# A decode attention kernel: the mask of the sliding-window units computed on chip from the identity, in place of two software-queued DMAs

## Chip, cores and metric

One core of a Trainium2 chip runs the whole program; the other cores are idle. The metric is the device time of one execution in microseconds (us), as the median over several executions. One run profiled by the hardware profiler goes with each kernel.

## The reference

Two independent decode attentions, A and B, with one query token for each of 4 batches, 32 query heads on 8 key/value heads, head size 128 and a cache of 8192 positions. A uses the whole cache, B its last 2048 positions. The outputs are concatenated.

```python
def _B_ref(x, k_cache, v_cache, wq, wo):          # A: the same without the window
    W = min(4096, max(256, Sk // 4))              # 2048
    q = (x @ wq).reshape(B, Sq, Hq, Dh) ...
    k = jnp.repeat(k_cache[:, :, Sk - W:, :], rep, axis=1)
    v = jnp.repeat(v_cache[:, :, Sk - W:, :], rep, axis=1)
    p = _softmax(jnp.einsum("bhqd,bhkd->bhqk", q, k) * (Dh ** -0.5), axis=-1)
    o = jnp.einsum("bhqk,bhkd->bhqd", p, v)
    return o ... @ wo                             # out: (4, 1, 1024) bf16
```

## The kernel before

The work is cut into 20 units: 4 of B, one for each batch, then 16 of A, one for each batch and pair of key/value heads. For every unit, SyncE loads 4.19 MB of K and 4.19 MB of V; TensorE transposes K (line 283), multiplies the scores, VectorE and ScalarE make the softmax, TensorE multiplies by V. K and V have two buffers each, so a load is issued as soon as the unit before the last has released its buffer.

In the K layout used here, a partition of the score tile belongs to one of two heads of a pair. Before the maximum over the partitions is taken, the columns of the other head are pushed to -1e30 by adding a mask. For A (MASKA) the two kinds of partitions are the lower and the upper half, which memsets can write. For B (MASKB) they alternate, even and odd. The kernel before wrote the rows into a helper tile MK in halves and let two DMAs from GpSimd's queue (software-queued: an instruction on GpSimd writes their descriptors) spread the rows over every second partition:

```python
def dve_addmask(u):                                     # first reader of the mask
    ...
    return dve.tensor_tensor(out=M1m[:, 0:n], in0=..., in1=MASK[P][:, 0:n], op=AluOpType.add)
    # waits: the scores' maximum, and in unit 0 also ("mk", 1), ("mka",)

def pool_mask0(pool):
    mkv = MK[:, :].rearrange("p (g s h) -> p g s h", g=NSEG, s=2)
    pool.memset(mkv[0:64, :, 0, :], 0.0)
    pool.memset(mkv[0:64, :, 1, :], -BIG)
    pool.memset(mkv[64:128, :, 0, :], -BIG)
    return pool.memset(mkv[64:128, :, 1, :], 0.0)
op("pool", pool_mask0, inc=("mk0",))
# ... pool_mask1 (MASKA), pool_setup0 (ones, zeros of RQ, OT_sb, oacc, PT, Wo_sb),
#     pool_setup1 (the identities ident and identf by affine_select), pool_perm

def dve_msk(dve):
    idv = ident[0:NR, 0:NR].rearrange("p (h b) -> p h b", h=C)
    dve.tensor_reduce(out=MSK[:, :], in_=idv, axis=AX.X, op=AluOpType.max)
    return dve.tensor_reduce(out=SEL[:, :], in_=idv.rearrange("p h b -> p b h"), axis=AX.X, op=AluOpType.max)
op("dve", dve_msk, waits=[("setup",)], inc=("msk",))
for sh in range(2):
    ...                                                 # destination: every second partition of MASKB
    def mfn(pool, dst_ap=dst_ap, sh=sh):
        return pool.dma_start(out=dst_ap, in_=MK[64 * sh:64 * sh + 64, :])
    op("pool", mfn, waits=[("mk0",)], inc=("mk", sh))
```

The set-up of the queries waits for the identity too: TensorE transposes x with it, projects x with WQ, and the first V load is issued when the B part of WQ, which lies in V's buffer, has been used.

Of the kernel before, what the change touches and what calls it, by code (L numbers as in the profile page):

```python
# [7 lines left out]
F32 = mybir.dt.float32  # L8
I32 = mybir.dt.int32
ACTF = mybir.ActivationFunctionType  # L10
AX = mybir.AxisListType
# [3 lines left out]
def bass_concat_heads__gqa_block_cached__sliding_block_cached__decode_kernel(  # L15
# [18 lines left out]
    REP = HQ // HKV  # L34
# [4 lines left out]
    NSEG = 4  # L39
    TS = NT // NSEG  # L40
    C = 2 * REP
# [4 lines left out]
    BIG = 1.0e30  # L46
# [13 lines left out]
    WQ = [A_wq, B_wq]  # L60
# [12 lines left out]
    with ExitStack() as es:  # L73
        block = es.enter_context(nc.Block())

        def sb(name, shape, dt):
            return es.enter_context(nc.sbuf_tensor(name, shape, dt))
# [4 lines left out]
        def sm(name):  # L82
            return es.enter_context(nc.semaphore(name))
# [6 lines left out]
        ident = sb("ident", [128, 128], BF16)  # L90
# [3 lines left out]
        RQ = [sb("RQ%d" % P, [128, Bn, NSEG, 2, 2 * C], BF16) for P in range(2)]  # L94
        RQc = sb("RQc", [128, 2, NSEG, 2, 2 * C], BF16)
        permE = sb("permE", [128, 2, 2, 64], BF16)
        MK = sb("MK", [128, NSEG * C], F32)
        MASK = [sb("MASKA", [128, C], F32), sb("MASKB", [128, NSEG * C], F32)]
        M1 = sb("M1", [128, NSEG * C], F32)
        M1m = sb("M1m", [128, NSEG * C], F32)  # L100
# [14 lines left out]
        ORx = sb("ORx", [C * Bn, C, C, 128 // C], BF16)  # L115
        MSK = sb("MSK", [C * Bn, C], BF16)
        SEL = sb("SEL", [C * Bn, Bn], BF16)
        OL = sb("OL", [128, C, Bn], BF16)
        oacc = sb("oacc", [Bn, D], F32)
        osb = sb("osb", [Bn, 2, D], BF16)  # L120
# [5 lines left out]

        names = ["k0", "k1", "kh", "v0", "v1", "vl0", "vl1", "vl2", "vl3", "vl4", "wl0", "wl1", "wl2", "wl3", "wl4", "wl5", "wl6", "wl7", "x0", "x1", "w0", "w1", "wo",
                 "out0", "out1", "out2", "Tq", "Td", "Ta", "S", "PV", "Ed", "Ea", "Eq", "vs", "sub", "exp", "otr", "otp",
                 "ocp", "Ef", "fin0", "fin1", "ar1", "SM", "msk", "pset", "setup", "pm0", "pm1", "oc", "ocB", "mk0", "mk", "mka", "perm", "rq"]
        sems = {n: sm("s_" + n) for n in names}  # L130

        K_sbf = K_sb.bitcast(F32)
# [6 lines left out]
        def sem_of(key):  # L139
            t = key[0]  # L140
            if t in ("K", "Kh"):
                return sems["k%d" % (key[1] % 2)]
            if t in ("V", "Vh"):
                return sems["v%d" % (key[1] % 2)]
            if t == "T":
                j = jobs[key[1]]
                return sems["Tq" if j["turn"] is None else "Td" if j["eng"] == "dve" else "Ta"]
            if t == "pm":
                return sems["pm%d" % key[2]]
            if t == "KH":  # L150
                return sems["kh"]
            if t in ("VL", "WL", "x", "out", "fin"):
                return sems["%s%d" % (t.lower(), key[1])]
            if t == "WQ":
                return sems["w%d" % key[1]]
            if t == "E":
                if jobs[key[1]]["turn"] is None:
                    return sems["Eq"]
                return sems["Ed"] if jobs[key[1]]["eng"] == "dve" else sems["Ea"]
            return sems["vs" if t in ("max", "maxc", "sum", "rcp", "os") else t]  # L160

        DMA_KEYS = ("K", "Kh", "KH", "V", "Vh", "VL", "WL", "x", "out", "WQ", "wo", "mk")

        plan = {e: [] for e in ("sp", "pe", "act", "dve", "pool")}
        turn = [None]
# [1 line left out]
        def op(eng, fn, waits=(), inc=None, bump=None):  # L167
            waits = list(waits)
            if not (eng == "pe" and turn[0] is not None):
                waits = [w for w in waits if w is not None]  # L170
            t = turn[0] if eng == "pe" or (eng in ("dve", "act") and turn[0] is not None and turn[0] >= T0P) else None
            plan[eng].append(dict(fn=fn, waits=waits, inc=inc, turn=t, bump=bump))
# [4 lines left out]
        def new_job(kind, eng):  # L177
            idx = len(jobs)
            step = 2 if kind == "OT" else 1
            bank = (jobs[-1]["bank"] + step) % NBK if jobs else 0  # L180
            jobs.append(dict(kind=kind, idx=idx, bank=bank, prev=bank_last.get(bank), eng=eng, turn=turn[0]))
            bank_last[bank] = idx
            return idx
# [7 lines left out]
        def kbank(idx):  # L191
            return KTB[jobs[idx]["bank"]]
# [180 lines left out]
        def pe_job_OL(tn):  # L373
            idx = ol_idx[tn] = new_job("OL", "dve")
            bk = kbank(idx)

            def fn(pe):
                ins = None
                for r in range(C):
                    ins = pe.matmul(out=bk[:, r * Bn:(r + 1) * Bn], lhsT=ORx[:, r, :, :].rearrange("p o i -> p (o i)"),  # L380
                                    rhs=SEL[:, :], start=True, stop=True)
                return ins
            op("pe", fn, waits=[("E", ot_idx[tn]), bankfree(idx)], inc=("T", idx))

            def efn(dve):
                return dve.tensor_copy(out=OL[:, :, :].rearrange("p r b -> p (r b)"), in_=bk[:, 0:NR])
            return dict(eng="dve", fn=efn, waits=[("T", idx)], inc=("E", idx))

        def pe_job_OPJ(tn):
# [3 lines left out]
            def fn(pe):  # L393
                ins = None
                for i in range(C):
                    ins = pe.matmul(out=bk[0:Bn, 0:D], lhsT=OL[:, i, :], rhs=Wo_sb[:, i, :],  # L396
                                    start=(i == 0), stop=(i == C - 1))
# [9 lines left out]
        def ncol(u):  # L407
            return NSEG * C if units[u]["P"] == 1 else C
# [21 lines left out]
        def dve_addmask(u):  # L430
            n, P = ncol(u), units[u]["P"]

            def fn(dve):
                return dve.tensor_tensor(out=M1m[:, 0:n], in0=M1[:, 0:n] if P == 1 else M1c[:, :], in1=MASK[P][:, 0:n], op=AluOpType.add)  # L434
            return dict(eng="dve", fn=fn, waits=[("max", u, 1) if P == 1 else ("maxc", u)] + ([("mk", 1), ("mka",)] if u == 0 else []), inc=("pm", u, 0))

        def pool_ar1(u):
            n = ncol(u)
# [80 lines left out]
                w.append(("otr", 2 * tn - 2))  # L519
            return dict(eng="pool", fn=lambda pool: pool.tensor_copy(out=OTp[:, :, :], in_=OT_sb[:, P, q, :, :]), waits=w, inc=("otp", tn))  # L520

        def pool_mask0(pool):
            mkv = MK[:, :].rearrange("p (g s h) -> p g s h", g=NSEG, s=2)
            pool.memset(mkv[0:64, :, 0, :], 0.0)
            pool.memset(mkv[0:64, :, 1, :], -BIG)
            pool.memset(mkv[64:128, :, 0, :], -BIG)
            return pool.memset(mkv[64:128, :, 1, :], 0.0)
        op("pool", pool_mask0, inc=("mk0",))

        def pool_mask1(pool):  # L530
            pool.memset(MASK[0][0:64, 0:REP], 0.0)
            pool.memset(MASK[0][0:64, REP:C], -BIG)
            pool.memset(MASK[0][64:128, 0:REP], -BIG)
            return pool.memset(MASK[0][64:128, REP:C], 0.0)
        op("pool", pool_mask1, inc=("mka",))

        def pool_setup0(pool):
# [6 lines left out]
            pool.memset(oacc[:, :], 0.0)  # L544
            pool.memset(PT[:, :, :], 0.0)
            return pool.memset(Wo_sb[:, :, :], 0.0)
        op("pool", pool_setup0, waits=[("mk0",), ("mka",)], inc=("pset",))

        def pool_setup1(pool):
            ins = pool.affine_select(out=ident[:, :], in_=onesb[:, :], pattern=[[1, 128]],  # L550
# [12 lines left out]
        op("pool", pool_perm, waits=[("setup",)], inc=("perm",))  # L563
        def dve_msk(dve):
            idv = ident[0:NR, 0:NR].rearrange("p (h b) -> p h b", h=C)
            dve.tensor_reduce(out=MSK[:, :], in_=idv, axis=AX.X, op=AluOpType.max)
            return dve.tensor_reduce(out=SEL[:, :], in_=idv.rearrange("p h b -> p b h"), axis=AX.X, op=AluOpType.max)
        op("dve", dve_msk, waits=[("setup",)], inc=("msk",))
        for sh in range(2):
            m0 = MASK[1][:, :]  # L570
            pstm = m0.ap[0][0]
            dst_ap = bass.AP(tensor=m0.tensor, offset=m0.offset + sh * pstm, ap=[[2 * pstm, 64], [1, NSEG * C]])

            def mfn(pool, dst_ap=dst_ap, sh=sh):
                return pool.dma_start(out=dst_ap, in_=MK[64 * sh:64 * sh + 64, :])
            op("pool", mfn, waits=[("mk0",)], inc=("mk", sh))

        def dma(dst, src):
            def fn(e):
# [33 lines left out]
        assert pc == NC  # L613
        AFTER = {("S", 2): ("OT",), ("S", 5): ("OL",)}

        for u in range(NU):
# [6 lines left out]
            def anchored(d):  # L623
                extra.setdefault(at, []).append(d)
            for tok in TOK:
# [15 lines left out]
                if odd and tok in AFTER:  # L641
                    kind = AFTER[tok][0]
                    anchored({"OT": pe_job_OT, "OL": pe_job_OL}[kind](tn))

# [9 lines left out]
            if units[u]["P"] == 0:  # L654
                add(dve_maxc(u))
            add(dve_addmask(u))
            if u >= 1:
                add(dve_sum(u - 1))
# [108 lines left out]
        for u in range(1, NU + 1):  # L767
# [4 lines left out]
            if u % 2 == 0 and tn in pieces:  # L772
                P, q = pieces[tn]
# [21 lines left out]
        for eng in plan:  # L795
            for o in plan[eng]:
# [5 lines left out]
                if o["inc"] is not None:  # L802
                    key = o["inc"]
                    sem = sem_of(key)
                    amt = 16 if key[0] in DMA_KEYS else 1
                    counters[sem.name] = counters.get(sem.name, 0) + amt
# [114 lines left out]
        def _(pool):  # L921
            emit("pool", pool)


# [1 line left out]
_INS = ['A_x', 'A_k_cache', 'A_v_cache', 'A_wq', 'A_wo', 'B_x', 'B_k_cache', 'B_v_cache', 'B_wq', 'B_wo']  # L926
_OUTS = [((4, 1, 1024), 'bfloat16')]
# [23 lines left out]
```

## Time and profile before

| | before |
|---|---|
| time, median of 3 (range) | 439.1 us (439.0 to 439.85) |
| span of the profiled run | 437.7 us |
| bytes read from HBM | 184.56 MB |
| share of SyncE's load queue in 16 DMA engines | 99.1% |
| busy: TensorE, VectorE, ScalarE, GpSimd | 84%, 48%, 45%, 7% |
| mask B landed, mask B first read | about 28.4 us, 49.7 us |

The strip of load rates in 40 slices of the span is level from the second slice to the last but one. The line of the chain of work that ended last:

```profile
PE 51%; DMA 43%; issue 2%; DVE 1%; SPq 1%; PEld 1%; ACT 0%; PEldq 0%
```

It names TensorE (PE) first.

### The profile page before, as it was taken

How to read it: one execution, taken by the hardware profiler on the slowest of the kernel's cores; microseconds unless marked ns; L12 is line 12 of the kernel's file. 1: busy time of each engine (PE TensorE's matmuls, PEld its weight loads, DVE VectorE, ACT ScalarE, POOL GpSimd, SP SyncE). 2: the span in 40 equal slices, each digit the busy share in tenths (PEclk: the TensorE clock that was granted, in tenths of full speed). 3: DMA queues.
4: the chain of work that ended last, by engine and by line, in shares of the span. 5: the costliest groups of instructions: out<-in, count | busy, mean ns of one | idle time of the engine just before them, and what ended most of it. 6: DMA issues, size and time to landing. Idle time of an engine off the chain costs nothing.

```text
span 437.7 us, 15534 instructions
## 1 busy us (share of the span) xinstructions
PE 365.7 (84%) x7174; PEld 338.4 (77%) x7184; DVE 209.5 (48%) x404; ACT 194.9 (45%) x249; POOL 29.0 (7%) x96
## 2 busy tenths in 40 slices
PE   0078998998998959895989598969888996989986
PEld 0068897997996949795979588868878786979975
DVE  0004555664564634563456347525653563455651
ACT  1024474473663625371735254424544462636530
POOL 7110000000000000000000000000100000000000
PEclk9999999999999988998999899969996998899999
DMA  8999999999999999999999999999999999999996
GB/s 339 425 424 416 430 414 431 416 442 410 444 431 431 421 442 431 431 431 431 431 431 431 431 431 427 436 429 431 416 446 431 431 432 431 431 431 422 440 407 245
DMA packets 11348, 184.75 MB, mean 422 GB/s; under 512 B 1300, under 2 KB 2376, under 8 KB 2632
## 3 DMA queue, kind: packets, MB, share of 16 engines
q1 hardware_dynamic: 11248, 184.56, 99.1%
q8 instruction: 8, 0.13, 0.1%
q14 instruction: 4, 0.03, 0.0%
q0 software_dynamic: 64, 0.02, 0.0%
q10 hardware_dynamic: 24, 0.01, 0.0%
HBM read 184.56 MB, written 0.01 MB: 422 GB/s over the span
## 4 chain that ended last, share of the span: by engine, by line
PE 51%; DMA 43%; issue 2%; DVE 1%; SPq 1%; PEld 1%; ACT 0%; PEldq 0%
DMA K_sb<-in_A_k_cache_dram 29%; PE KT L283 25%; PE OT L338 10%; DMA K_sb<-in_B_k_cache_dram 7%; DMA V_sb<-in_A_v_cache_dram 7%; PE SB L322 4%; PE SA L322 4%; PE KT L396 4%; PE SA L350 1%; SPq L580 1%; DVE oacc L404 1%; PE KT L338 1%; PEld OT L338 1%; ACT KT_sb L299 0%; PE KT L263 0%
## 5 line engine op out<-in xcount | busy, mean ns | idle before, releaser
L283 PE MATMUL KT<-identf,K_sb 128*128 128x128 f32 x1280 | 208.1, 296 | 42.9 <-DMA K_sb<-in_A_k_cache_dram 30.4
L299 ACT ACTIVATE KT_sb<-KT 128x1024 bf16<-128x1024 bf16 (+1 forms) x192 | 165.0, 881 | 119.8 <-PE KT L283 119.8
L283 PEld LDWEIGHTS KT<-identf,K_sb 128*128 128x128 f32 x1280 | 148.0, 150 | 48.1 <-DMA K_sb<-in_A_k_cache_dram 31.4
L299 DVE COPY KT_sb<-KT 128x512 int32<-128x512 int32 x160 | 110.4, 690 | 131.9 <-PE KT L283 130.5
L338 PE MATMUL OT<-PT,V_sb 128*128 128x64 bf16 x2560 | 78.1, 193 | 1.6 <-issue 0.9
L338 PEld LDWEIGHTS OT<-PT,V_sb 128*128 128x128 bf16 x2560 | 75.9, 98 | 1.8 <-issue 1.0
L469 ACT ACTIVATE PT<-Dt 128x512 bf16<-128x512 f32 x40 | 24.6, 630 | 84.0 <-DVE Dt L458 84.0
L322 PEld LDWEIGHTS SA<-RQc,KT_sb 128*128 128x128 bf16 x1280 | 57.0, 98 | 2.3
L322 PEld LDWEIGHTS SB<-RQc,KT_sb 128*128 128x128 bf16 x1280 | 51.0, 97 | 7.9 <-issue 4.4
L322 PE MATMUL SA<-RQc,KT_sb 128*128 128x16 bf16 x1280 | 56.4, 170 | 0.0
L322 PE MATMUL SB<-RQc,KT_sb 128*128 128x16 bf16 x1280 | 52.9, 170 | 0.0
L420 DVE TENSOR_REDUCE M<-SB 128x8 f32<-128x512 f32 (+1 forms) x20 | 13.8, 691 | 50.1 <-PE SB L322 50.1
L441 POOL PARTITION_ALL_REDUCE MB<-M1m x20 | 7.7, 385 | 333.7 <-DVE M1m L434 333.7
L396 PE MATMUL KT<-Wo_sb,OL 128*4 128x512 bf16 x80 | 18.9, 379 | 0.0
L201 PE MATMUL KT<-ident,x_sb 4*128 4x4 bf16 x8 | 0.5, 169 | 20.8 <-POOL identf L552 20.8
L201 PEld LDWEIGHTS KT<-ident,x_sb 4*128 4x128 bf16 x8 | 0.4, 111 | 21.0 <-issue 21.0
L476 DVE TENSOR_REDUCE LB<-SA 128x8 f32<-128x512 f32 (+1 forms) x20 | 13.7, 684 | 2.8 <-PE SA L350 2.8
L458 DVE TENSOR_TENSOR Dt<-SA,MBm 128x512 f32<-128x512 f32 x20 | 13.8, 691 | 0.7
L367 DVE TENSOR_TENSOR ORx<-KT,MSK 32x1024 bf16<-32x1024 bf16 x10 | 12.1, 1212 | 3.3 <-PE KT L362 3.3
L420 DVE TENSOR_REDUCE M<-SA 128x8 f32<-128x512 f32 (+1 forms) x20 | 13.6, 681 | 0.0
L458 DVE TENSOR_TENSOR Dt<-SB,MBm 128x512 f32<-128x512 f32 x20 | 13.6, 680 | 0.0
L350 PE MATMUL SA<-PT,onesb 128*128 128x128 bf16 x168 | 12.8, 218 | 0.0
(74 smaller groups left out, 119.5 us busy)
## 6 DMA issues: line engine op xcount, KB each, us to landing
K_sb<-in_A_k_cache_dram SPq DMA_DIRECT2D x15, 4096.0 KB, 22.5
V_sb<-in_A_v_cache_dram SPq DMA_DIRECT2D x15, 4096.0 KB, 30.6
K_sb<-in_B_k_cache_dram SPq DMA_DIRECT2D x8, 2048.0 KB, 23.9
V_sb<-in_B_v_cache_dram SPq DMA_DIRECT2D x16, 1024.0 KB, 18.7
V_sb<-in_B_wq_dram SPq DMA_DIRECT2D x1, 4096.0 KB, 12.4
V_sb<-in_A_wq_dram SPq DMA_DIRECT2D x1, 4096.0 KB, 22.4
Wo_sb<-in_B_wo_dram SPq DMA_DIRECT2D x4, 1024.0 KB, 12.0
K_sb<-in_A_k_cache_dram SPq DMA_DIRECT2D x2, 2048.0 KB, 17.9
```

The costliest lines, as they stand in the source:

```text
L283: ins = pe.transpose(out=bkf[:, pi * 128:(pi + 1) * 128], in_=K_sbf[:, slot, t0:t0 + 2, :].rearrange("p t d -> p (t d)"), identity=identf[ ...
L299: ins = e.tensor_copy(out=d, in_=r) if eng == "dve" else e.activation(out=d, in_=r, func=ACTF.Copy)
L322: ins = pe.matmul(out=stb[:, t % NTH * C:(t % NTH + 2) * C], lhsT=ktv[:, pi, :, e], rhs=RQc[:, u % 2, t // TS, e, :], start=(e == 0), stop ...
L338: ins = pe.matmul(out=otb[:, s * NW:s * NW + w], lhsT=V_sb[:, slot, t, :], rhs=PT[:, slot, t * C:t * C + w], start=(j == 0), stop=(j == n ...
L350: ins = pe.matmul(out=SA[u % 2][:, s * NM:(s + 1) * NM], lhsT=onesb[:, :], rhs=PT[:, u % 2, c0:c0 + NM], start=(i == 0), stop=(i == n - 1))
L367: return dve.tensor_tensor(out=ORx[:, :, :, :], in0=bk[0:NR, 0:128].rearrange("p (i o r) -> p r o i", o=1, r=C).broadcast_to([NR, C, C, 12 ...
L396: ins = pe.matmul(out=bk[0:Bn, 0:D], lhsT=OL[:, i, :], rhs=Wo_sb[:, i, :], start=(i == 0), stop=(i == C - 1))
L420: return dve.tensor_reduce(out=M1[:, h * n:(h + 1) * n].rearrange("p (s h) -> p s h", h=C), in_=bank[:, :].rearrange("p (s j h) -> p s h j ...
L441: return pool.partition_all_reduce(MB[:, 0:n], M1m[:, 0:n], channels=128, reduce_op=ReduceOp.max)
L458: return dve.tensor_tensor(out=Dt[:, h * NTH * C:(h + 1) * NTH * C].rearrange("p (s j h) -> p s j h", s=Sh, h=C), in0=bank[:, :].rearrange ...
L469: return act.activation(out=PT[:, u % 2, a:b], in_=Dt[:, a:b], func=ACTF.Exp, scale=scale)
L476: return dve.tensor_reduce(out=LB[:, 0:n].rearrange("p (s h) -> p s h", h=C), in_=SA[u % 2][:, 0:NSEG * NM].rearrange("p (s j h) -> p s h ...
```

## The change

The intent is to take two transfers, their helper tile and their memsets out of the start-up: EO holds, for each partition, whether it is even or odd, as the maximum of its identity row over the even and over the odd columns; one GpSimd instruction makes the mask of it, (EO - 1) x 1e30.

```diff
-        MK = sb("MK", [128, NSEG * C], F32)
+        EO = sb("EO", [128, 2], F32)
...
-        op("pool", pool_mask0, inc=("mk0",))          # and its four memsets
-        op("pool", pool_setup0, waits=[("mk0",), ("mka",)], inc=("pset",))
+        op("pool", pool_setup0, waits=[("mka",)], inc=("pset",))
...
         def dve_msk(dve):
+            dve.tensor_reduce(out=EO[:, :], in_=ident[:, :].rearrange("p (i s) -> p s i", s=2), axis=AX.X, op=AluOpType.max)
             dve.tensor_reduce(out=MSK[:, :], ...)
...
-        for sh in range(2): ...                        # the two DMAs
+        def pool_mask2(pool):
+            return pool.tensor_scalar(out=MASK[1][:, :].rearrange("p (g s h) -> p g s h", g=NSEG, s=2),
+                                      in0=EO[:, :].rearrange("p (g s h) -> p g s h", g=1, h=1).broadcast_to([128, NSEG, 2, REP]),
+                                      scalar1=-1.0, scalar2=BIG, op0=AluOpType.add, op1=AluOpType.mult)
+        op("pool", pool_mask2, waits=[("msk",)], inc=("mkb",))
```

The first reader waits for "mkb" in place of "mk".

More of the change, by code (lines that the diff above doesn't have):

```diff
@@ L128, in bass_concat_heads__gqa_block_cached__sliding_block_cached__decode_kernel @@
                  "out0", "out1", "out2", "Tq", "Td", "Ta", "S", "PV", "Ed", "Ea", "Eq", "vs", "sub", "exp", "otr", "otp",
-                 "ocp", "Ef", "fin0", "fin1", "ar1", "SM", "msk", "pset", "setup", "pm0", "pm1", "oc", "ocB", "mk0", "mk", "mka", "perm", "rq"]
+                 "ocp", "Ef", "fin0", "fin1", "ar1", "SM", "msk", "pset", "setup", "pm0", "pm1", "oc", "ocB", "mkb", "mka", "perm", "rq"]
         sems = {n: sm("s_" + n) for n in names}
@@ L160, in sem_of @@
             return sems["vs" if t in ("max", "maxc", "sum", "rcp", "os") else t]
-        DMA_KEYS = ("K", "Kh", "KH", "V", "Vh", "VL", "WL", "x", "out", "WQ", "wo", "mk")
+        DMA_KEYS = ("K", "Kh", "KH", "V", "Vh", "VL", "WL", "x", "out", "WQ", "wo")
         plan = {e: [] for e in ("sp", "pe", "act", "dve", "pool")}
@@ L434, in fn @@
                 return dve.tensor_tensor(out=M1m[:, 0:n], in0=M1[:, 0:n] if P == 1 else M1c[:, :], in1=MASK[P][:, 0:n], op=AluOpType.add)
-            return dict(eng="dve", fn=fn, waits=[("max", u, 1) if P == 1 else ("maxc", u)] + ([("mk", 1), ("mka",)] if u == 0 else []), inc=("pm", u, 0))
+            return dict(eng="dve", fn=fn, waits=[("max", u, 1) if P == 1 else ("maxc", u)] + ([("mkb",), ("mka",)] if u == 0 else []), inc=("pm", u, 0))
         def pool_ar1(u):
@@ L520, in pool_otp @@
             return dict(eng="pool", fn=lambda pool: pool.tensor_copy(out=OTp[:, :, :], in_=OT_sb[:, P, q, :, :]), waits=w, inc=("otp", tn))
-        def pool_mask0(pool):
-            mkv = MK[:, :].rearrange("p (g s h) -> p g s h", g=NSEG, s=2)
-            pool.memset(mkv[0:64, :, 0, :], 0.0)
-            pool.memset(mkv[0:64, :, 1, :], -BIG)
-            pool.memset(mkv[64:128, :, 0, :], -BIG)
-            return pool.memset(mkv[64:128, :, 1, :], 0.0)
-        op("pool", pool_mask0, inc=("mk0",))
         def pool_mask1(pool):
@@ L568, in bass_concat_heads__gqa_block_cached__sliding_block_cached__decode_kernel @@
         op("dve", dve_msk, waits=[("setup",)], inc=("msk",))
-        for sh in range(2):
-            m0 = MASK[1][:, :]
-            pstm = m0.ap[0][0]
-            dst_ap = bass.AP(tensor=m0.tensor, offset=m0.offset + sh * pstm, ap=[[2 * pstm, 64], [1, NSEG * C]])
-            def mfn(pool, dst_ap=dst_ap, sh=sh):
-                return pool.dma_start(out=dst_ap, in_=MK[64 * sh:64 * sh + 64, :])
-            op("pool", mfn, waits=[("mk0",)], inc=("mk", sh))
+        def pool_mask2(pool):
[3 more added lines that the diff above has]
+        op("pool", pool_mask2, waits=[("msk",)], inc=("mkb",))
         def dma(dst, src):
```

## The prediction

> **What bounds the kernel now.** The program reads its whole input once, so I looked first at the strip of the span in 40 slices and the table of DMA queues on the page.
>
> ```profile
> DMA  8999999999999999999999999999999999999996
> GB/s 339 425 424 416 430 414 431 416 442 410 444 431 431 421 442 431 431 431 431 431 431 431 431 431 427 436 429 431 416 446 431 431 432 431 431 431 422 440 407 245
> q1 hardware_dynamic: 11248, 184.56, 99.1%
> ...
> q0 software_dynamic: 64, 0.02, 0.0%
> ```
>
> The DMA engines are busy in every slice, and from the second slice to the last but one the rate stays between 407 and 446 GB/s, mostly 431. Queue q1, the loads issued by SyncE, carries 184.56 MB and fills 99.1% of 16 engines' span. Queue q0 carries the two mask transfers that the change takes away. The only slices that are low are the first and the last: a ramp at the start and a tail after the stream.
>
> The chain of work that ended last looks at first as if TensorE were the bound. It puts 51% on PE and 43% on DMA. That share is misleading, because on the chain a TensorE stretch and a DMA stretch can both be running while the stream goes on. I therefore asked whether the stream ever runs dry, with the timeline of SyncE's issues:
>
> ```profile
> 0.80 0.39 SPq L580 DMA_DIRECT2D V_sb<-in_B_wq_dram  x1
> 1.24 0.42 SPq L580 DMA_DIRECT2D V_sb<-in_A_wq_dram  x1
> 1.71 2.62 SPq L580 DMA_DIRECT2D K_sb<-in_B_k_cache_dram  x4
> 25.03 2.48 SPq L580 DMA_DIRECT2D V_sb<-in_B_v_cache_dram  x4
> 41.27 6.34 SPq L580 DMA_DIRECT2D K_sb<-in_B_k_cache_dram  x2
> ...
> 309.19 0.33 SPq L580 DMA_DIRECT2D Wo_sb<-in_A_wo_dram  x1
> ...
> 411.30 16.57 SPq L580 DMA_DIRECT2D Wl_sb<-in_A_wo_dram  x8
> 435.95 0.28 SPq L580 DMA_DIRECT2D out_dram<-osb  x1
> ```
>
> By 25.03 us, 2 x 4096 KB and 4 x 2048 KB have been issued, 16.8 MB. At the rates of the first slices (10.94 us each: 339 x 10.94 + 425 x 10.94 + 424 x 3.15) 9.7 MB have been moved, so some 7 MB wait; counted by the packets in the trace it is 7.36 MB, or 17 us of work. I did the same count, bytes issued less bytes of finished packets, at every issue up to 423 us. It never falls below 3.24 MB (at 309.19 us), that is 7.5 us of work at 431 GB/s. No pause of more than 0.05 us without a load packet in flight exists before the last load ends. So the time is: 1.8 us until the first packet, 432.8 us of stream (1.8 to 434.6 us; 184.55 MB at a mean 426 GB/s), and 3.1 us for the last output (to 437.7 us). The measured 439.1 us is the span of 437.7 us and some 1.4 us around it.
>
> The rest is the place of the change. First the instructions that touch the mask of the B units, then the start-up of the other engines:
>
> ```profile
> L434 DVE TENSOR_TENSOR M1m<-M,MASKB x4: 191/192/192, 49.7 to 102.5; 128x32 f32<-128x32 f32 x4
> L575 POOL DMA_DIRECT2D MASKB<-MK x2: 527/688/848, 21.5 to 22.3; - x2
> DMA to landing us min/median/max: 5.7/6.4/7.1
> ```
>
> ```profile
> 0.80 0.10 POOL L524 MEMSET MK<- 64x16 f32 x1 [0.29 <-POOLq L936]
> ...
> 1.18 0.09 POOL L531 MEMSET MASKA<- 64x4 f32 x1
> ...
> 20.14 0.28 POOL L550 TENSOR_SCALAR_AFFINE_SELECT ident<-onesb 128x128 bf16<-128x128 bf16 x1 [11.22 <-issue]
> ...
> 20.71 0.17 DVE L566 TENSOR_REDUCE MSK<-ident 32x8 bf16<-32x32 bf16 x1 [20.71 <-POOL identf L552]
> ...
> 26.55 0.29 POOL L310 COPY RQc<-RQ 128x128 bf16<-128x128 bf16 x1 [3.71 <-ACT RQ L250]
> ...
> 34.04 3.28 PEld L283 LDWEIGHTS KT<-identf,K_sb 128*128 128x128 f32 x16 [2.87 <-DMA K_sb<-in_B_k_cache_dram]
> ```
>
> The mask lands by about 28.4 us (the end of the last q0 packet) and its first reader starts at 49.68 us. That is 21 us of slack before the change does anything. In the list of who waited for whom, nobody waited for MASKB's transfers. And the start-up as a whole ends in a wait for data: the K transposes begin at 34.04 us, as K lands.
>
> **What the Trainium skill says.** "DMA: Bandwidth & Descriptors", section "Where 436 GB/s comes from", puts the ceiling of the transfer fabric at 435 GB/s. The 431 GB/s of the steady slices agree; there is no spare rate for any compute change to use. The same page, "Issuing engines are not separate DMA queues", says that transfers from SyncE, ScalarE and GpSimd run on the same 16 engines and interleave. That fits the trace: the mask's packets lie between 25.5 and 28.4 us, among q1's. "Perfetto Trace Analysis", section "DMA Instruction — SWDGE (GPSIMD)", says that the profiled end of such an instruction is the end of descriptor generation, not of the data. The trace agrees: 0.53 and 0.85 us for the two instructions, 5.7 and 7.1 us to landing. "GPSIMD Engine Reference", section "2.1 Instruction dispatch", says that the first call of a freshly loaded kernel pays about 6 us without a visible instruction. The trace has a silent gap of 11.22 us before the first affine select, longer than that[...]; whether the added GpSimd instruction pays anything alike is a rival below.
>
> **The change part by part.**
> - *Removed from the DMA engines:* 32 packets of 512 B at 27 ns and 32 of 4 B at 9 ns, by the durations of nearly all of them in the trace: 1.15 us over 16 engines, 0.07 us of each. This is the only part on the path that sets the end. Worth -0.07 us.
> - *Removed from GpSimd, descriptors:* 2 issues, 1.39 us in the timeline (21.46 to 22.85 us). The next GpSimd work, the RQc copy, waits for ScalarE until 26.55 us. Off the path, 0.
> - *Removed from GpSimd, MK:* 4 memsets, from 0.80 to 1.18 us. Everything up to the identity may come 0.38 us earlier, if the 11.22 us gap keeps its length, and with it the Q projection and the V load now issued at 25.03 us. With 7.36 MB before it in the queue that moves no byte earlier. 0.
> - *Added on VectorE:* EO, a maximum over 128x128 bf16 into 128x2. Estimate from two reductions in this trace: 32 elements a partition 0.17 us, 512 elements 0.69 us, so 1.08 ns an element and 0.17 + 96 x 1.08 ns = 0.27 us. It goes ahead of MSK and SEL, so their semaphore comes 0.27 us later, near 21.2 us (before any gain of 0.38 us). TensorE waits for it only after its last set-up matmul at about 31.4 us, and then waits for K until 34.0. 0.
> - *Added on GpSimd:* one tensor_scalar writing 128x32 f32. The 128x32 copy (OTp) takes 0.21 us; I take 0.2 to 0.3 us, near 21.5 us, in time that the descriptors filled. 0.
> - *Moved:* the mask is ready near 21.8 us in place of 28.4. Its reader still comes at 49.7 us, released by the last scores. 0. VectorE's two waits there change their semaphore, not their number.
>
> Sum: -0.07 us on a time of 439.1 us, rounded to 439.0 us.
>
> **The rivals.**
> - *A new wait at start-up.* If the new tensor_scalar pays a silent first-call cost of 6 to 11 us, GpSimd reaches the first RQc copy at 28 to 33 us in place of 26.55. The first score matmuls run at 37.5 us, so even the worst is covered. If it pushed them out by some microseconds, the first stage would release K buffers later, with 4.7 MB in the queue at 41.27 us, 11 us of work. Time 439.0 to 439.1. For it: the 11.22 us gap. Against it: the page's gap is of the first call, and this instruction follows affine selects that ran without another gap.
> - *The identity on the path.* Start-up has long idle stretches (TensorE waits 20.8 us for the identity), which looks like gain: 0.38 us earlier would make 438.7. Against it: the queue of issued loads does not run dry, so only a shift of the stream itself counts.
> - *A disturbance that goes.* If GpSimd's descriptors or its small packets slow the loads more than their own duration, removing them could give some tenths. The windows 20 to 21 us (295 GB/s) and 21 to 22 us (360 GB/s) are low, but mostly before these packets, and 22 to 26 us is at 377 to 454. At the most 0.3 us: 438.8.
> - *A shift of buffers.* Taking MK out moves later tensors in SBUF. I see nothing in the trace on which that would act; 0, with a small chance of the unknown.
>
> **Range and chances.** The three runs before span 439.0 to 439.85 us and the profiled one took 439.48, so noise of about 0.8 us, mostly upwards, is ten times the effect. From 439.0: 438.4 below (the two small rivals together, -0.4, and a little noise), 439.9 above (the highest run before). A 2% change would be 8.8 us, and the largest thing that I can take away from the stream is 0.07 us; a loss of that size needs the queue to run dry, which needs at least 7.5 us of new delay somewhere. Chances: faster 0.01, same 0.98, slower 0.01.
>
> **What would show it right or wrong.** After: no q0 row; HBM read still 184.56 MB and q1 at about 99% of the span; steady slices at 431 GB/s; the affine select near 19.8 us; EO about 0.27 us; the GpSimd instruction 0.2 to 0.3 us with no silent gap before it; K transposes of the first unit still near 34.0 us, behind DMA; the addition of the mask still near 49.7 us. It would be wrong if a slice in the middle fell well under 431 GB/s, if a wait for the new mask stood ahead of the addition at 49.7 us, or if a gap of over 10 us opened on GpSimd before the first RQc copy.

## The result, and the profile after

| | before | after |
|---|---|---|
| time, median of 6 (range) | 439.24 us (438.99 to 439.85) | 439.41 us (439.15 to 439.92) |
| ratio, 95% interval | | 1.0003 (0.999 to 1.0016) |
| the same in a later sample, 9 and 5 runs | 439.67 us | 439.43 us, ratio 0.9998 (0.9984 to 1.0012) |
| span of the profiled run | 437.7 us | 437.3 us |

A ratio is the mean time of one kernel's fast runs over the mean of the other's fast runs of the same rounds, so it is not quite the ratio of the medians beside it. In both samples the two kernels are the same within 0.16%, or 0.7 us.

The page of the changed kernel, first the rates in 40 slices (GB/s), then the one queue that matters and the bytes:

```profile
GB/s 342 427 418 418 427 416 432 416 439 411 449 432 432 421 440 432 432 432 432 432 432 432 432 432 427 436 429 432 412 448 432 432 432 432 432 432 412 445 405 256
...
q1 hardware_dynamic: 11248, 184.56, 99.1%
...
HBM read 184.56 MB, written 0.01 MB: 422 GB/s over the span
```

The strip is that of before to within 11 GB/s in every slice, and to within 3 in most, the number of load packets and bytes is the same, and the row of the software queue (q0) is gone. The start-up in order of time (start, duration, engine, line, operation, and in brackets the idle time before it and what ended it):

```profile
19.57 0.28 POOL L542 TENSOR_SCALAR_AFFINE_SELECT ident<-onesb 128x128 bf16<-128x128 bf16 x1 [11.10 <-issue]
...
20.14 0.28 DVE L558 TENSOR_REDUCE EO<-ident 128x2 f32<-128x128 bf16 x1 [20.14 <-POOL identf L544]
20.17 0.77 POOL L553 COPY permE<-ident 128x64 bf16<-128x64 bf16 x4
...
21.04 0.22 POOL L563 TENSOR_SCALAR MASKB<-EO 128x32 f32<-128x32 f32 x1
...
24.46 2.97 SPq L570 DMA_DIRECT2D V_sb<-in_B_v_cache_dram  x4
...
25.98 0.29 POOL L310 COPY RQc<-RQ 128x128 bf16<-128x128 bf16 x1 [4.73 <-ACT RQ L250]
...
34.16 0.93 PEld L283 LDWEIGHTS KT<-identf,K_sb 128*128 128x128 f32 x5 [3.91 <-DMA K_sb<-in_B_k_cache_dram]
```

The identity comes 0.57 us earlier (19.57 against 20.14 us), and so do the first V load (24.46 against 25.03 us) and the RQc copy. But the first K transposes still wait for K to land, and they start at 34.16 us against 34.05 us before. The 0.57 us has only made their wait longer: 3.91 us against 2.87 us. The mask is there at 21.3 us, 7 us earlier than the transfers brought it. Its reader is not earlier (instructions on MASKB: minimum, median, maximum in ns, then first and last start in us):

```profile
L434 DVE TENSOR_TENSOR M1m<-M,MASKB x4: 191/191/193, 50.4 to 103.2; 128x32 f32<-128x32 f32 x4
...
L563 POOL TENSOR_SCALAR MASKB<-EO x1: 219/219/219, 21.0 to 21.0; 128x32 f32<-128x32 f32 x1
```

It even runs 0.7 us later than before (50.4 against 49.7 us), because two of TensorE's groups of four transposes, at 37.9 and 39.0 us, took 1.09 us each where they had taken 0.95 and 0.64 us. That differs from run to run (1.09 twice in after_again, 0.63 and 0.64 us in two_queues), and no run shows why. The delay is made up at the first long wait for data. The chain that ended last, before and then after, where TensorE first waits for a K load of the A units:

```profile
141.35 22.96 DMA K_sb<-in_A_k_cache_dram
164.35 3.68 PE KT L283 x16
```

```profile
142.05 22.07 DMA K_sb<-in_A_k_cache_dram
164.16 3.67 PE KT L283 x16
```

The load is issued 0.70 us later after the change, and it ends the wait 0.19 us earlier: when an engine is ready decides when a load joins the queue, and the queue decides when it lands.

### The profile page after: what moved, and what is told of

Same layout as the page of the kernel before. It is cut to its first block, busy times and chain, and to the rows that moved or that the text cites. A ratio compares the mean times of both kernels' runs of the same rounds, so it can differ in the third digit from the quotient of the medians.

```text
span 437.3 us, 15529 instructions
## 1 busy us (share of the span) xinstructions
PE 366.3 (84%) x7174; PEld 338.7 (77%) x7184; DVE 209.6 (48%) x405; ACT 195.0 (45%) x249; POOL 27.6 (6%) x91
## 3 DMA queue, kind: packets, MB, share of 16 engines
q1 hardware_dynamic: 11248, 184.56, 99.1%
## 4 chain that ended last, share of the span: by engine, by line
PE 51%; DMA 43%; issue 2%; DVE 1%; SPq 1%; PEld 1%; ACT 1%; PEldq 0%
DMA K_sb<-in_A_k_cache_dram 29%; PE KT L283 25%; PE OT L338 10%; DMA K_sb<-in_B_k_cache_dram 7%; DMA V_sb<-in_A_v_cache_dram 7%; PE SB L322 4%; PE SA L322 4%; PE KT L396 4%; PE SA L350 1%; SPq L570 1%; DVE oacc L404 1%; PE KT L338 1%; PEld OT L338 1%; ACT KT_sb L299 1%; PE KT L263 0%
## 5 line engine op out<-in xcount | busy, mean ns | idle before, releaser
L283 PE MATMUL KT<-identf,K_sb 128*128 128x128 f32 x1280 | 208.5, 297 | 42.3 <-DMA K_sb<-in_A_k_cache_dram 28.8
L476 DVE TENSOR_REDUCE LB<-SA 128x8 f32<-128x512 f32 (+1 forms) x20 | 13.7, 683 | 2.8 <-PE SA L350 2.8
L367 DVE TENSOR_TENSOR ORx<-KT,MSK 32x1024 bf16<-32x1024 bf16 x10 | 12.1, 1211 | 3.8 <-PE KT L362 3.8
```

The source lines that it names most:

```text
L283: ins = pe.transpose(out=bkf[:, pi * 128:(pi + 1) * 128], in_=K_sbf[:, slot, t0:t0 + 2, :].rearrange("p t d -> p (t d)"), identity=identf[ ...
L367: return dve.tensor_tensor(out=ORx[:, :, :, :], in0=bk[0:NR, 0:128].rearrange("p (i o r) -> p r o i", o=1, r=C).broadcast_to([NR, C, C, 12 ...
L476: return dve.tensor_reduce(out=LB[:, 0:n].rearrange("p (s h) -> p s h", h=C), in_=SA[u % 2][:, 0:NSEG * NM].rearrange("p (s j h) -> p s h ...
```

## The experiments

The theory: SyncE's stream of loads sets the time; the start-up and the mask lie beside it as long as the stock of loads (bytes of the loads issued, less bytes of finished packets) does not run out; the change can win only the DMA time of two small transfers. The rivals: TensorE sets it (51% of the chain); the start-up counts; the software-queued transfers disturb the loads by more than their own packets. All kernels are the changed kernel with one edit, and all gave correct results. The ratios are to the kernel before, run on the same chip.

### more_mask_dmas: what does such a transfer cost?

```diff
+            if u in (4, 6, 8, 10, 12, 14):             # behind the unit's last GpSimd work
+                for i in range(16):                    # 64 rows x 128 B into every second partition of JK
+                    op("pool", ... pool.dma_start(out=JK..., in_=MASK[1][64 * (i % 2):64 * (i % 2) + 64, :]), ...)
```

> The changed kernel with 96 more software-queued transfers of the size of a mask half (48 pairs, each pair as large as the one that the change took away), 16 each in units 4, 6, 8, 10, 12 and 14, at a place where GpSimd is otherwise idle. Theory (the load stream sets the time; a pair costs only the time of its own packets on the DMA engines): between 0.79 MB at 431 GB/s = 1.8 us and 48 x 0.072 us = 3.5 us longer than the changed kernel, so 441.2 to 442.9 us. Rival (a pair disturbs the loads by more than its own packets, 0.3 us as the prediction allowed at most): +14 us, 454 us. If transfers hide entirely: 439.4 us.

Measured: 443.56 us against 439.3 us, ratio 1.0095 (1.008 to 1.0111), 4.2 us more for 48 pairs. The queues of this kernel:

```profile
q1 hardware_dynamic: 11248, 184.56, 98.4%
q0 software_dynamic: 3072, 0.79, 0.8%
```

A pair costs 4.2 / 48 = 0.09 us (0.07 to 0.10 by the interval), a little above the range from packets alone (0.04 to 0.07 us) and far from the 0.3 us that the rival allowed. The trace shows where the rest may lie: q0's packets take 3.5 us of 16 engines, as expected, and the load packets of q1 take 1.2 us of 16 engines more than in the changed kernel's trace. So the two transfers that the change removed were worth about 0.09 us, if they cost in the start-up what these cost in the middle. That is about an eighth of the 0.7 us that the samples can resolve.

### ident_first: the identity six microseconds earlier

```diff
+        op("pool", pool_ones, waits=[("mka",)], inc=("ones",))        # onesf, onesb, dummy only
-        op("pool", pool_setup1, waits=[("pset",)], inc=("setup",))
+        op("pool", pool_setup1, waits=[("ones",)], inc=("setup",))
         op("pool", pool_perm, waits=[("setup",)], inc=("perm",))
+        op("pool", pool_setup0, waits=[("mka",)], inc=("pset",))      # the large memsets, now behind
...                                                     # their readers now wait for ("pset",)
```

> The changed kernel with the large memsets of GpSimd moved behind the identity, so that the identity is there at about 12.5 us instead of 19.6 us, and the first V load is issued near 17 us, when the weights have landed at 13.2 us, instead of 24.5 us. Theory: loads issued earlier only stand in the queue longer; no change, 439.4 us within 0.5. Rival (the start-up to the identity counts in the time, wholly or in part; then the 0.57 us by which the change brought the identity forward was a gain that something else ate): -3 to -7 us, 432 to 436 us.

Measured: 439.24 us, ratio 0.9999 (0.9986 to 1.0013).

```profile
13.62 0.28 POOL L544 TENSOR_SCALAR_AFFINE_SELECT ident<-onesb 128x128 bf16<-128x128 bf16 x1 [12.08 <-issue]
...
18.51 2.52 SPq L573 DMA_DIRECT2D V_sb<-in_B_v_cache_dram  x4
...
34.43 0.71 PEld L283 LDWEIGHTS KT<-identf,K_sb 128*128 128x128 f32 x4 [5.79 <-DMA K_sb<-in_B_k_cache_dram]
```

The identity came 6 us earlier than in the changed kernel (not 7: the silent gap grew to 12.08 us), the first V load was issued at 18.51 us, and the K transposes still began at 34.4 us, after a longer wait for K. The rival that the start-up counts is out, and with it the idea that the change's 0.57 us was a gain that something else ate.

### ident_late3, ident_late7, ident_late10, ident_late21: how much delay the stock covers

One, two, three or six memsets of 3.5 us ahead of the identity, into a buffer that is loaded only near the end:

```diff
+        for i in range(n):                             # n = 1, 2, 3, 6
+            op("pool", lambda pool: pool.memset(Wl_sb[:, :, :], 0.0), waits=[("hold", i - 1)] if i else [("mka",)], inc=("hold", i))
-        op("pool", pool_setup0, waits=[("mka",)], inc=("pset",))
+        op("pool", pool_setup0, waits=[("mka",), ("hold", n - 1)], inc=("pset",))
```

> The changed kernel with two more memsets of 3.5 us on GpSimd ahead of the identity: identity at about 26.6 us. Theory: the count of issued loads less landed ones stays over 1 MB (first V issue near 31.5 us with some 4.7 MB waiting, at the smallest 1.3 MB near 59 us), so the stream does not dry up and the time stays at 439.4 us within 0.5. Rival (start-up counts one for one): +7 us, 446 us.

> As the run before with six such memsets: identity at about 40.6 us, first K transposes near 52 us instead of 34.2 us, 18 us later. Theory: the smallest stock of waiting loads in the first units is about 3.0 MB or 7 us, so only what exceeds it is lost: 18 - 7 = +11 us, between 447 and 453 us, with a visible hole in the load rate between 40 and 75 us. Rival (one for one): +21 us, 460 us. Rival (start-up never matters): 439.4 us.

Measured: 441.05 us (ratio 1.0044, 1.003 to 1.0057) with two, where the theory said no change; 454.28 us (1.0345, 1.0329 to 1.0361) with six, above the range of the theory. A control was wanted for whether the memsets themselves did harm, and a point between:

> The changed kernel with one memset of 3.5 us ahead of the identity: identity near 23.1 us, the set-up matmuls of TensorE done near 34 us, so the K transposes begin at most 0.5 us later than the 34.2 us at which K lands. Both forms of the theory: no change, 439.4 us within 0.5. Rival (the 1.75 us that two memsets cost came from GpSimd's memsets or the late first V load as such): +0.9 us, 440.2 us.

> The changed kernel with three such memsets: identity near 30.2 us, K transposes about 7.7 us later. Two forms of the theory. (1) The whole stock of 3.0 MB can be used up before time is lost, which gives 7.7 - 7.0 = +0.7 us at most, 440 us; then the +1.75 us of two memsets (K transposes 4.2 us later) is unexplained. (2) Time is lost as soon as the stock falls below some 2 MB, because single engines run dry before the sum does; a line through the two runs so far (4.2 us later: +1.75; 18 us later: +15) starts at 2.5 us, which gives 7.7 - 2.5 = +5 us, 444.5 us.

| memsets | identity, us | first K transposes, us | smallest stock at an issue near 60 us, MB | time, us | ratio to before |
|---|---|---|---|---|---|
| 0 (the changed kernel, first sample) | 19.6 | 34.2 | 3.00 | 439.41 | 1.0003 |
| 1 | 23.5 | 36.2 | 1.92 | 439.09 | 0.9995 |
| 2 | 26.8 | 39.5 | 1.06 | 441.05 | 1.0044 |
| 3 | 29.3 | 42.5 | 0.44 | 443.21 | 1.0100 |
| 6 | 40.9 | 53.3 | 0 | 454.28 | 1.0345 |

The columns before the times come from the profiled run of each kernel; where time was lost, that was the fastest run of its sample (440.43, 442.04 and 452.26 us). The stock is counted from the trace, as in the prediction, at the issue of the second unit's V load (55 to 62 us); with six memsets it is 0 already at the first V load. The transposes begin later by 5.3 us with two memsets and by 19.1 us with six, not by the 4.2 and 18 us that the expectations name: those are the delays of the K load that follows (from 41.99 to 46.16 and 60.15 us).

One memset moved the transposes by 2.0 us, more than the expected 0.5 us, and cost nothing. From two on, time is lost. The load rate, in windows of 10 us (only the last two columns matter here: DMA share and GB/s), of the changed kernel and then with three memsets:

```profile
60.00:70.00 10.00, 10.00 (x214) 8.68 (x213) 5.36 (x11) 4.39 (x9) 0.43 (x1) 1.00 0.99 411
```

```profile
60.00:70.00 10.00, 10.00 (x187) 9.88 (x184) 6.01 (x9) 7.91 (x15) 0.00 (x0) 1.00 0.89 352
```

And the strip of the kernel with six memsets (slices of 11.3 us):

```profile
DMA  8996868999999999999999999999999999999996
GB/s 350 421 434 287 325 258 328 432 416 440 428 432 434 422 425 442 437 425 428 437 434 416 440 440 428 425 429 440 431 425 431 437 410 446 431 440 413 440 412 245
```

With six memsets four slices are low. Against 431 GB/s they lack (144 + 106 + 173 + 103) x 11.26 us = 5.9 MB, or 13.7 us, and the span of this run is 13.0 us over that of the changed kernel (450.3 against 437.3 us). So a delay does cost time, and the hole that it leaves in the stream accounts for the loss to within a microsecond. With three memsets the 7.0 us of stock was not all usable; the loss was about 4 us, near the 5 us of form (2) and far from 0.7 us. So form (1) of the theory falls. Form (2) holds in size, but its limit of some 2 MB is too high: 1.92 MB cost nothing here, nor did 1.44 MB (at 128.32 us) in filler12 below.

Why time is lost with bytes still outstanding can be read from the trace in part. It does not name the engine of a packet, but it counts packets in flight: 16.1 or 16.2 on average in each microsecond from 54 to 72 us of the changed kernel, about one for each of the 16 DMA engines. With two memsets the mean is 14.5 from 61 to 63 us, though 3.6 MB or more were issued and not landed; with three it is 9.4 from 62 to 64 us. So engines stand idle before the sum is 0. One reason shows with six memsets: a load issued into the empty queue, at 45.81 and at 60.15 us, has its first packet 1.3 us later, so the stock at an issue has to last at least that long, and 0.44 MB last 1.0 us at 431 GB/s. With two, three and six memsets, idle engines add up to 0.2, 1.1 and 10.6 us and packets that took longer to 0.4, 1.5 and 2.1 us, of spans longer by 1.0, 2.9 and 13.0 us. The 0.4 us left over with two memsets is within the spread of the spans (437.1 to 437.9 us for the changed kernel); why packets took longer is not shown.

### mask_late: the mask 16 us later

```diff
-        op("pool", pool_mask2, waits=[("msk",)], inc=("mkb",))
...                                                     # in unit 0, behind the copy for unit 1:
+                for i in range(3):
+                    op("pool", lambda pool: pool.memset(Wl_sb[:, :, :], 0.0), waits=[("hold", i - 1)] if i else [], inc=("hold", i))
+                op("pool", pool_mask2, waits=[("msk",), ("hold", 2)], inc=("mkb",))
```

> The changed kernel with the computation of the mask moved behind three memsets of 3.5 us each, to about 37.5 us: later than the transfers of the kernel before delivered it (28.4 us), still ahead of its first reader (50.4 us). Theory: 439.4 us within 0.5, no wait for the mask. Rival (when the mask is there matters, so that its arrival 7 us earlier was worth something): +2 us or more. The first all-reduce may come later, if GpSimd has another silent gap of some 11 us between the mask and it; up to 3 us of that is absorbed by the stock of loads.

Measured: 439.17 us, ratio 0.9993 (0.9979 to 1.0007). The instructions on MASKB in this kernel:

```profile
L434 DVE TENSOR_TENSOR M1m<-M,MASKB x4: 191/192/193, 50.2 to 103.1; 128x32 f32<-128x32 f32 x4
...
L563 POOL TENSOR_SCALAR MASKB<-EO x1: 220/220/220, 37.6 to 37.6; 128x32 f32<-128x32 f32 x1
```

The mask written at 37.6 us, 16.6 us later than in the changed kernel, leaves its reader at 50.2 us and the time as it was. The all-reduce behind the reader came at 50.57 us, not late. This run is also the control for the memsets: three of them, behind the identity, cost nothing.

### more_bytes: 2.1 MB that nobody reads

```diff
         kv_load("K", 0)
+        op("sp", dma(XB[:, :], WQ[1].rearrange("(p c) n -> p (c n)", p=128)[:, 0:8192]), inc=("xb",))
```

> The changed kernel with one more load of 2.10 MB issued by SyncE behind the first K loads, into a buffer that nobody reads. Theory (stream-bound): + 2.10 MB / 431 GB/s = +4.9 us, 444.3 us, even though no engine waits for that buffer. Rival (TensorE bounds, as its 51% of the chain suggests, and the loads have slack): 0 to +1 us.

Measured: 444.17 us against 439.67 us, ratio 1.0102 (1.0087 to 1.0118).

```profile
q1 hardware_dynamic: 11392, 186.66, 99.1%
```

4.5 us more, with 3.8 to 5.2 us from the interval; the estimate of 4.9 us lies in it. The share of the queue is still 99.1%: the span grew with the bytes.

### filler12: more work for TensorE

```diff
-    NFILL = 3
+    NFILL = 12
```

> The changed kernel with 12 instead of 3 filler matmuls of 512 columns in every even unit: 9 x 10 = 90 more matmuls, at some 0.2 us each (three take about 0.6 us) 19 us more work for TensorE, spread over the kernel. Theory (stream-bound; TensorE has 16% idle time, in which this fits): 439.4 us within 0.7; a lower granted clock is possible and would add a little. Rival (TensorE bounds, as its 51% of the chain suggests): +10 to +19 us, 449 to 458 us.

Measured: 439.59 us, ratio 1.0002 (0.9989 to 1.0016). TensorE's busy time on the page of the changed kernel, and in this one:

```profile
PE 366.3 (84%) x7174; PEld 338.7 (77%) x7184; DVE 209.6 (48%) x405; ACT 195.0 (45%) x249; POOL 27.6 (6%) x91
```

```profile
PE 379.5 (87%) x7274; PEld 342.1 (78%) x7274; DVE 209.8 (48%) x405; ACT 194.5 (44%) x249; POOL 27.7 (6%) x91
```

13.2 us more of busy time on TensorE, none of it in the time. The fillers themselves took the 19 us expected (27.5 us for 120, against 8.1 us for 30 in after_again), but the K transposes took 6.1 us less than in the changed kernel (202.4 against 208.5 us); why is not shown. The granted clock did not fall (0.981 against 0.961). TensorE is not the bound, whatever its share of the chain. But its work is free only out of the stock: the fillers took the smallest stock at an issue down to 1.44 MB, from 3.00 MB in the changed kernel.

### after_again, the control

> The changed kernel once more, as the control on the chip of the three runs beside it. Theory: 0.07 us faster than before, not to be told from 0; the ratio to before between 0.998 and 1.002. A rival in which the earlier identity or the missing transfers count would give a ratio of 0.998 or less in every sample.

Measured: 439.43 us, ratio 0.9998 (0.9984 to 1.0012). That the point estimate falls on the expected 0.07 to 0.09 us is luck: that of the first sample has the other sign (1.0003, +0.13 us), and the interval is seven to nine times as wide to either side. It shows only that no gain of more than 0.7 us is there.

### two_queues: an attempt at a faster version

```diff
-        for P in (1, 0):
+        for P in (1,):
             op("sp", dma(V_sb[:, 1 - P, ...]), inc=("WQ", P))
+        op("act", dma(V_sb[:, 1, ...], WQ[0]...), inc=("WQ", 0))      # behind the two x loads
```

> The changed kernel with the weights of the A units loaded from ScalarE's queue behind the two x loads, so that two queues fill the DMA engines in the first microseconds. In the kernel before, 7.18 MB have landed by 20 us, which 431 GB/s would need 16.7 us for: 3.3 us are lost, 1.8 of them before the first packet. If the rest is lost for want of issued loads, up to -1.5 us, 438 us; if the ramp is the DMA engines' own, no change, 439.4 us. A gain here would make this a version faster than both kernels.

Measured: 439.18 us, ratio 0.9997 (0.9984 to 1.001). No gain, and by 20 us 7.23 MB have landed on all queues, as in the kernel before: a second queue does not quicken the first microseconds. What makes them slow stays open. No version here beats the two kernels.

## Why the prediction was right

**The bound.** Right, and shown from both sides: bytes count at the rate of the stream (more_bytes, 4.5 us for 2.1 MB), while TensorE's work does not count (filler12).

**Removed from the DMA engines, -0.07 us.** The mechanism is right; measured on 48 pairs it is 0.09 us a pair. This is below what the samples of the change resolve, so the sign of the change's own effect is not shown.

**Removed from GpSimd, and the identity earlier by 0.38 us, worth 0.** The shift was 0.57 us, since the set-up memsets ended 0.45 us earlier and the silent gap was 0.12 us shorter. Its worth of 0 is shown by ident_first, with a shift ten times as large.

**Added: EO 0.27 us, tensor_scalar 0.2 to 0.3 us.** 0.28 and 0.22 us. Between the permE copies and the tensor_scalar lies 0.1 us, so the rival of a silent first-call cost is out. MSK and SEL came behind EO and nobody waited for them.

**The mask earlier, worth 0.** It was ready at 21.3 us (predicted 21.8) and not read before 50.4 us; mask_late shows that even 37.6 us is early enough.

**The margin.** Here the prediction was too generous. It said that a loss of 8.8 us (2%) "needs the queue to run dry, which needs at least 7.5 us of new delay". No run contradicts that for so large a loss, but the reading behind it, that all of the stock is slack, is wrong. The runs show a loss of 1.75 us when TensorE's K transposes were 5.3 us late, with 1.06 MB still outstanding, and none when they were 2.0 us late, with 1.92 MB. The usable margin is between 2.0 and 5.3 us and not 7. The change came nowhere near it, so the chances were not affected.

**A shift of buffers.** This rival was not tested by itself. Whatever it does lies within the 0.7 us in which the two kernels agree.

## What to carry to other kernels

When the load rate is level through the whole profile and the stock of issued loads never runs out, only bytes and packets count: judge a change by what it takes off the stream, not by the idle time or the waits that it removes elsewhere. Waits at the start-up and a large share of an engine on the chain are no evidence by themselves; the cheap test is to add work to that engine, and the cheap test of the stream is to add bytes. And do not spend the whole stock as slack: here time was lost when a megabyte was still outstanding at the next issue, and a new load had its first packet only 1.3 us after its issue.

## What the Trainium skill lacked or had wrong

- "DMA: Bandwidth & Descriptors", section "Where 436 GB/s comes from", says without a condition that for transfers from HBM a limit of about 358 GB/s a core binds, though it calls its own 425 GB/s for 16 MB near the fabric rate, and though the note just above that section gives 358 for both cores of a pair streaming. With the other cores idle, this core read 431 to 432 GB/s from HBM in the level slices, next to the 435 GB/s fabric ceiling that the same section gives. The condition belongs in the sentence.
- "GPSIMD Engine Reference", section "2.1 Instruction dispatch", puts the silent cost of a first call at about 6 us. Ahead of the first affine select the runs show 10.1 to 12.1 us, and the tensor_scalar after it paid none (0.1 us). No run here shows what the gap consists of.
- No page says what a small software-queued transfer costs a saturated stream: 0.09 us for two of 8 KB (48 pairs, 4.2 us), against 5.7 and 7.1 us from issue to landing of the two in the kernel before.
- No page says how many bytes must be outstanding to keep the stream full: with 1.92 and 1.44 MB (ident_late3, filler12) as the smallest stock at an issue nothing was lost, with 1.06 MB 1.75 us, with 0.44 MB 4 us.
